# Windowed attention, then a sine-squared feed-forward layer: the squares of four groups of batch 0's first product move to GpSimd

## Chip, cores and metric

The kernel runs on one core of a Trainium2 chip. The metric is the device time of one execution in microseconds (us), as the median of several runs. A profile of one more execution shows what each engine did: TensorE (PE, its weight loads PEld), VectorE (DVE), ScalarE (ACT), GpSimd (POOL) and SyncE (SP, which issues transfers).

## What is computed

Eight batches of eight heads, 576 positions and 64 columns go through attention in which a position sees its neighbours within 32 and eight global positions; the result (4608 tokens x 512) goes through a layer with 2048 inner columns and a sine-squared activation.

```python
B, H, S, D = q.shape                       # 8, 8, 576, 64
scores = scale * np.matmul(q, k.transpose(0, 1, 3, 2))
mask = (np.abs(pos[:, None] - pos[None, :]) <= 32) | is_global[:, None] | is_global[None, :]
attn = softmax(np.where(mask, scores, -1e9))
x = (attn @ v).transpose(0, 2, 1, 3).reshape(B * S, H * D)
h = x @ w_in                               # 4608 x 2048
s = np.sin(alpha * h)
g = h + s * s / (alpha + 1e-09)
return (g @ w_out).astype(np.float32)
```

## The kernel before

The work goes batch by batch, in an order that is written out by hand (a manual schedule: each engine executes its instructions in the order of the program text, and waits at the head of its queue for what it needs). For batch b there is a stage of attention (`phase_a`, `attention`), then the first product with the activation (`gemm1`), and the second product (`gemm2`), whose matrix products are handed out piece by piece (`fill`) among the next batch's attention and first product.

`gemm1(b)` loops over 16 groups `nt` of 128 inner columns. For each group TensorE makes eight products (four row blocks of the weights, two halves of the 576 columns) into a PSUM bank pair; the groups take the bank pairs zn, zr and zd in turn, so that the product of group nt reuses the bank of group nt - 3. Then four steps follow: ScalarE's sine (L1162, bank to `sb`), the square (`sb` to `s2`: on ScalarE at L1165 if the group is in `on_act`, otherwise on VectorE at L1167), and VectorE's update (L1168), which multiplies the square by `recipT`, adds the bank and writes `H2`. With the update the bank is free again. `sb` and `s2` have three buffers each. For batch 0 `on_act` is `ON_ACT_FIRST`, the groups 1, 3, 5, 7, 9, 11, 13 and 14.

During batch 0's first product, the queries and keys of batch 1 are brought into their layout as well. Behind the products of the groups in `TURNED` (4, 7, 10, 13) TensorE transposes one pair of heads (`turn_lying`, L630) into the two spare PSUM banks zo. At the start of the groups in `PLACED` (5, 8, 11, 14), ahead of that group's sine in each queue, these banks are copied out (`place_lying`): the keys by VectorE (L637, into KX), the queries by ScalarE (L642, into QX). The next transposes into a bank wait for its copy.

GpSimd's queue in this stage holds, from group 1 on, two casts of the gathered rows of global keys and queries (L717, each waits for its gather), the issue of a transfer that casts batch 2's queries (L334, `cast_heads`), and from group 13 on three copies of global columns (`place_globals`, L374 and L377), which wait for two casts that VectorE makes behind group 12's transposes (`turn_kq`, L731). In the next stage its first instruction is a copy of one element that paces transfers (L353) and waits for the first masked weights E.

The next stage begins with seven products of `gemm2(0)` (L1220) into the spare bank from which the last keys were copied, followed by scores (L814) into a new bank pair in zr's place and into zd, exponentials on ScalarE (L822) and masks on VectorE (L831).

```python
ON_ACT_FIRST = (1, 3, 5, 7, 9, 11, 13, 14)
TURNED, PLACED, GLOBALS = (4, 7, 10, 13), (5, 8, 11, 14), 12
START = 7                                   # gemm2's products ahead of the next batch's scores
```

Of the kernel before, what the change touches and what calls it, by code (L numbers as in the profile page):

```python
# [10 lines left out]
ALU = mybir.AluOpType  # L11
# [238 lines left out]
def kernel(  # L250
# [11 lines left out]
    nc = tc.nc  # L262
# [68 lines left out]
    def cast_heads(b, src, name):  # L331

        cast[b, name] = dramp.tile([S, H, D], DT.bfloat16, name=name)
        nc.gpsimd.dma_start(out=cast[b, name][:], in_=src[b].rearrange("h s d -> s h d"))  # L334
# [16 lines left out]
    def pace(src):  # L351

        nc.gpsimd.tensor_copy(out=seen[0 : src.shape[0]], in_=src)  # L353

    def turn_k(b, _):
        kd = cast[b, "kd"][:].rearrange("a i h d -> a (i h d)")
        nc.sync.dma_start_transpose(out=KXt[b % 2][:].rearrange("p i h d -> p (i h) d")[:, :, 0:KT], in_=kd)
# [24 lines left out]
    def globals_of(b, rows, y):  # L382

        q0 = QX[b % 2][rows, :, y, PAD : PAD + 4]
        return bass.AP(
            tensor=q0.tensor, offset=q0.offset, ap=[list(q0.ap[0]), [2 * QROW, NHP], [SEG, 7], [1, 4]]
        )
# [14 lines left out]
    def load_v(b):  # L402

        src = cast[b, "vd"][:].rearrange("(m a) h d -> a m (h d)", a=KT)
        for half in range(2):
            m0 = half * (NT6 - 1)
            nc.sync.dma_start(
                out=VX[b % 2][half * D : half * D + KT].rearrange("p m h d -> p m (h d)"),
                in_=src[:, m0 : m0 + NT6 + 1],
            )  # L410

    def load_vg(b):
        for r in (KT, D + KT):
            nc.sync.dma_start(
                out=VX[b % 2][r : r + NG].rearrange("p m h d -> p m (h d)"),
                in_=VGb[b::B][:, None, :].to_broadcast([NG, NT6 + 1, H * D]),
            )
# [74 lines left out]
    for t in (gidx8, gp64):  # L492
        nc.vector.memset(t[:].bitcast(DT.int32), 0)
    nc.sync.dma_start(
        out=g64[:],
# [4 lines left out]
    for t in (0, D):  # L500
        nc.sync.dma_start(out=gp64[t + KT : t + NK], in_=global_idx[:, None])
        nc.sync.dma_start(
            out=gidx8[t + KT : t + NK],
# [31 lines left out]
    for i, bits in enumerate((B - 1, D - 1, B * (NG - 1))):  # L535
        nc.vector.tensor_scalar(
            out=rowi[:, i : i + 1], in0=prow[:], scalar1=bits, scalar2=None, op0=ALU.bitwise_and
# [12 lines left out]
        out=rowf[0 : NG * B, 4:5], in0=rowf[0 : NG * B, 0:1], scalar=float(S), in1=rowf[0 : NG * B, 3:4], op0=ALU.mult, op1=ALU.add  # L550
# [4 lines left out]
        out=of_batch[:], in0=rowf[0 : NG * B, 0:1], scalar1=0.0, scalar2=None, op0=ALU.is_equal  # L555
    )
    nc.vector.tensor_scalar(
        out=pick[:], in0=place8[0 : NG * B], scalar1=rowf[0 : NG * B, 2:3], scalar2=of_batch[:, 0:1],
# [8 lines left out]
    def warm(z, n):  # L567
# [9 lines left out]
        out=KX[1][:, :, :, NK:D], in_=zero[:][:, None, None, :].to_broadcast([P, NHP, NT12, D - NK]), func=AF.Copy,  # L577
# [15 lines left out]
    for half in range(2):  # L593
# [12 lines left out]
        out=band[:], in0=qrel[:], scalar1=float(WIN * WIN) + 0.5, scalar2=None, op0=ALU.is_le  # L606
    )
    for e, c0 in ((0, PAD), (1, 40)):
        nc.vector.tensor_copy(
            out=band[:, e, :, c0 : c0 + 4], in_=iskey[:, :, None].to_broadcast([P, 2, 4])  # L610
# [3 lines left out]
        out=M2, in_=band[:].rearrange("p e x c -> p e (x c)")[:, None].to_broadcast([P, NT6 // 2, 2, WCOL])  # L614
# [20 lines left out]
    def place_lying(b, w, hp, z, copy):  # L635
        if w == 1:
            copy(  # L637
                out=KX[b][:, hp, :, 0:KT].rearrange("p i (q r) -> p i q r", r=NR),
                in_=z.rearrange("p (r i q) -> p i q r", i=NT12, r=NR),
            )  # L640
        else:
            copy(  # L642
                out=QX[b][:, hp, :, PAD : PAD + 6 * SEG].rearrange("p y (m c) -> p y m c", c=SEG)[
                    :, :, :, 4:
                ].rearrange("p y m (e a) -> p y m e a", a=NR // 2),
                in_=z.rearrange("p (a y m e) -> p y m e a", y=2, m=6, a=NR // 2),
            )
# [11 lines left out]
        out=first[:], in0=gf[:], scalar1=gpf[:, 0:1], scalar2=None, op0=ALU.not_equal  # L659
# [3 lines left out]
        out=later[:], in0=jrow[:], scalar1=pm, scalar2=float(-KT), op0=ALU.subtract, op1=ALU.is_ge  # L663
# [8 lines left out]
    for w, name in ((1, "k"), (0, "q")):  # L672
        for t in range(2):
            nc.tensor.matmul(
                out=pg[w][t * D : (t + 1) * D], lhsT=g0[name][:], rhs=identb[0 : NG * B, t : NG * B : 2],
# [6 lines left out]
        out=KX[0][:, :, :, KT:NK],  # L682
        in_=pg[1].rearrange("p (j h) -> p h j", h=NHP)[:, :, None, :].to_broadcast([P, NHP, NT12, NG]),
    )
    for y in range(2):
        act(
            out=globals_of(0, slice(0, P), y),
# [6 lines left out]
        out=far[:], in0=qpos[:], scalar1=float(WIN * WIN) + 0.5,  # L694
# [20 lines left out]
    def cast_globals_kq():  # L715
        for w, src in ((1, gk), (0, gq)):
            nc.gpsimd.tensor_copy(out=gkq[w][:], in_=src)  # L717
# [26 lines left out]
    def halves(z, W):  # L744
        c = columns(z, W)
        return [(c[:, lo:hi], lo, hi) for lo, hi in ((0, HALF), (HALF, W))]
# [335 lines left out]
    TURNED, PLACED, GLOBALS = (4, 7, 10, 13), (5, 8, 11, 14), 12  # L1082
# [14 lines left out]
    def gemm1(b):  # L1097


        while len(waiting) > 1:  # L1100
            fill(1)
        xT = xTs[b]
        r0 = (b % 2) * S
        more = b == B - 1
        W = SG if more else S
        hr = tc.alloc_tile_pool(name="hr", bufs=1, space=PSUM)
        hs = {}

        def chunks(nt, cs, parts=slice(0, 2)):
            if nt not in hs:  # L1110
                hs[nt] = (zn, None, zd)[nt % 3] or hr.tile([P, 2, 512], DT.float32, name="zr")
            h = hs[nt]
            for c in cs:
                for h_part, lo, hi in halves(h, W)[parts]:
                    nc.tensor.matmul(  # L1115
                        out=h_part, lhsT=w_in[:, c, nt * P : (nt + 1) * P], rhs=xT[:, c, lo:hi],
                        start=(c == 0), stop=(c == CT - 1), skip_group_check=True,
                    )

        on_act = (ON_ACT_FIRST, ON_ACT_SECOND, ON_ACT)[min(b, 2)]  # L1120
        for nt in range(NT):
            at_group[0] = (b, nt)
            if b == 0 and nt in PLACED:
                hp = PLACED.index(nt)
                for w, copy in ((1, nc.vector.tensor_copy), (0, nc.scalar.copy)):
                    place_lying(1, w, hp, spare_banks[w], copy)
            if b == 0 and nt == 1:
                cast_globals_kq()
                load_v(1)
                load_vg(1)  # L1130
                cast_heads(2, q, "qd")
            if 0 < nt and cast_at.get((b, nt)):
                pace(H2[0:1, nt - 1, r0 : r0 + 1])
                for piece in cast_at[b, nt]:
                    cast_one(*piece)
            if 0 < b and b + 1 < B and 0 < nt <= TURNS:
                turn_k(b + 1, nt - 1)
            if 0 < b and b + 1 < B and nt == (LATE if b == 1 else TURNS + 1):
                load_v(b + 1)
                load_vg(b + 1)  # L1140
            if b == 0 and nt == GLOBALS + 1:
                for part in range(3):
                    place_globals(1, part, nc.gpsimd.tensor_copy)
            if more and nt == SOON:
                put_globals(slice(0, SOON))
            if nt == 0:

                for n in range(2):
                    chunks(n, range(CT - 1), slice(0, 2 - more))
                for n in range(2 * more):  # L1150
                    chunks(n, range(CT - 1), slice(1, 2))
            chunks(nt, range(CT - 1, CT) if nt < 2 else range(CT))
            h = columns(hs[nt], W)
            fill((GROUP_LAST if more else PER_GROUP)[nt])
            if nt and copied[0] == (b, nt - 2):
                fill(AFTER_COPY)
            if b == 0 and nt in TURNED:
                turn_lying(1, TURNED.index(nt), spare_banks)
            if b == 0 and nt == GLOBALS:
                turn_kq()  # L1160
            sb = spool.tile([P, SG], DT.bfloat16, name="sb")
            nc.scalar.activation(out=sb[:, 0:W], in_=h, func=AF.Sin, scale=alphaT[:, nt : nt + 1])  # L1162
            s2 = spool.tile([P, SG], DT.bfloat16, name="s2")
            if nt in on_act:
                nc.scalar.activation(out=s2[:, 0:W], in_=sb[:, 0:W], func=AF.Square)  # L1165
            else:
                nc.vector.tensor_tensor(out=s2[:, 0:W], in0=sb[:, 0:W], in1=sb[:, 0:W], op=ALU.mult)  # L1167
            nc.vector.scalar_tensor_tensor(  # L1168
                out=H2[:, nt, r0 : r0 + W], in0=s2[:, 0:W], scalar=recipT[:, nt : nt + 1], in1=h,
                op0=ALU.mult, op1=ALU.add,  # L1170
            )
        hr.release()
        at_group[0] = None
# [106 lines left out]
    def fill(n):  # L1280
        while n and waiting:
            if next(waiting[0], None) is None:
                waiting.pop(0)
            else:
                n -= 1
# [111 lines left out]
```

## Time and profile before

| what | us |
|---|---|
| median of three runs | 338.68 (338.3 to 339.26) |
| the profiled execution, its own time | 338.49 |
| its span, first to last instruction | 336.8 |
| batch 0's first product: first sine to last update | 31.46 to 53.45 |
| mean granted TensorE clock | 0.996 of full speed |

In the profile's rows, a group is written as output<-inputs by the names of the program's tiles; "x8" is a count, and the bracket at the end of a timeline row gives the idle time of the engine before it and what ended it. Of the columns of a timeline the first is the start in us from the span's beginning, the second the duration. The engine columns of the table by stretches are busy time with the number of instructions. In a table of groups the two numbers behind the bar are total busy time in us and the mean in ns. Spans on GpSimd are rough.

### The profile page before, as it was taken

The numbers are of one execution on the slowest core, as the hardware profiler recorded it, in microseconds if no ns is written. First come the engines' busy times: TensorE is split into PE (matmuls) and PEld (weight loads), VectorE is DVE, ScalarE is ACT, GpSimd is POOL, SyncE is SP. The second block draws the span as 40 slices with busy tenths as digits, with TensorE's granted clock in tenths as the row PEclk, the third lists the DMA queues.
The fourth block names the chain that finished last, engine by engine and source line by source line (L and its number), as shares of the span: only waits on it lengthen the run. The fifth ranks groups of instructions, "written<-read, shape, count | busy, mean of one in ns | idle before, by whom it ended". The sixth has DMA issues, their size and how long they took to land.

```text
span 336.8 us, 11878 instructions
## 1 busy us (share of the span) xinstructions
PE 316.2 (94%) x4812; PEld 202.8 (60%) x4812; DVE 255.9 (76%) x488; ACT 277.1 (82%) x402; POOL 143.7 (43%) x296
## 2 busy tenths in 40 slices
PE   0778999999999999999999999999999999999993
PEld 0765765577556765667556755676567745665553
DVE  4885896887887788688877788778868888788930
ACT  6775888989998889988998889889898898889611
POOL 7983324349516670666355652487060000004500
PEclk9999999999999999999999999999999999999998
DMA  7999999999989998999969993899999311010232
GB/s 104 114 162 205 186 226 169 152 166 135 181 143 133 190 124 137 94 119 186 151 93 137 172 162 85 131 176 136 132 111 133 65 60 42 1 33 8 73 93 69
DMA packets 141942, 42.01 MB, mean 125 GB/s; under 512 B 126426, under 2 KB 136794, under 8 KB 141882
## 3 DMA queue, kind: packets, MB, share of 16 engines
q0 software_dynamic: 100096, 18.51, 71.1%
q1 hardware_dynamic: 41786, 22.69, 34.1%
q8 instruction: 38, 0.62, 0.8%
q14 instruction: 22, 0.18, 0.2%
HBM read 41.95 MB, written 20.77 MB: 186 GB/s over the span
## 4 chain that ended last, share of the span: by engine, by line
PE 87%; DVE 4%; ACT 3%; issue 2%; DMA 1%; POOL 1%; DVEq 0%; POOLq 0%
PE zo L1220 38%; PE zn L1115 14%; PE zr L1115 11%; PE zd L1115 10%; PE ring L814 4%; PE zd L862 4%; PE zn L862 2%; DVE H L1168 2%; DMA g0k<-in_k_dram,grow 1%; ACT sb L1162 1%; PE zn L814 1%; PE zr L862 1%; DVE recipT L712 1%; DVE s L1167 1%; PE zo L630 1%
## 5 line engine op out<-in xcount | busy, mean ns | idle before, releaser
L1220 PE MATMUL zo<-w_out,H 128*128 128x512 bf16 (+1 forms) x576 | 147.1, 377 | 0.3 <-DVE KX L637 0.3
L1115 PEld LDWEIGHTS <-w_in 128*128 128x128 bf16 x1024 | 100.1, 98 | 43.9 <-issue 8.3
L1220 PEld LDWEIGHTS <-H 128*128 128x128 bf16 x592 | 53.7, 98 | 46.2 <-issue 0.4
L1115 PE MATMUL zn<-xT,w_in 128*128 128x288 bf16 (+1 forms) x384 | 57.7, 290 | 1.6 <-DVE H L1168 1.4
L1115 PE MATMUL zr<-xT,w_in 128*128 128x288 bf16 x320 | 48.0, 288 | 0.3
L1168 DVE SCALAR_TENSOR_TENSOR H<-s,recipT,zn 128x576 bf16<-128x576 bf16 (+1 forms) x48 | 39.4, 822 | 10.4 <-ACT s L1165 6.5
L1162 ACT ACTIVATE sb<-zn,alphaT 128x576 bf16<-128x576 f32 (+1 forms) x48 | 35.7, 743 | 13.7 <-PE zn L1115 13.2
L1115 PE MATMUL zd<-xT,w_in 128*128 128x288 bf16 x320 | 46.3, 288 | 0.3 <-DVE H L1168 0.2
L822 ACT ACTIVATE E<-ring 128x720 bf16<-128x720 f32 x46 | 35.9, 780 | 8.3 <-PE ring L814 7.7
L1167 DVE TENSOR_TENSOR s<-sb 128x576 bf16<-128x576 bf16 (+1 forms) x70 | 32.6, 465 | 12.2 <-ACT sb L1162 12.0
L1165 ACT ACTIVATE s<-sb 128x576 bf16<-128x576 bf16 (+1 forms) x58 | 40.0, 689 | 1.8
L831 DVE TENSOR_TENSOR E<-E,MASKT 128x720 bf16<-128x720 bf16 x64 | 33.5, 529 | 7.6 <-ACT E L822 5.6
L1168 DVE SCALAR_TENSOR_TENSOR H<-s,recipT,zd 128x576 bf16<-128x576 bf16 (+1 forms) x40 | 32.9, 822 | 7.6 <-ACT s L1165 5.0
L1168 DVE SCALAR_TENSOR_TENSOR H<-s,recipT,zr 128x576 bf16<-128x576 bf16 (+1 forms) x40 | 32.9, 822 | 6.6 <-ACT s L1165 5.0
L344 POOL DMA_DIRECT2D kd<-in_k_dram x48 | 31.4, 657 | 10.4 <-issue 8.0
L1162 ACT ACTIVATE sb<-zd,alphaT 128x576 bf16<-128x576 f32 (+1 forms) x40 | 29.6, 740 | 5.2 <-PE zd L1115 5.1
L1162 ACT ACTIVATE sb<-zr,alphaT 128x576 bf16<-128x576 f32 (+1 forms) x40 | 29.6, 740 | 4.3 <-PE zr L1115 4.3
L1210 POOL COPY H<-H 128x11 bf16 (+1 forms) x16 | 7.2, 453 | 57.6 <-DVE H L1168 56.7
L346 POOL DMA_DIRECT2D vd<-in_v_dram x48 | 30.5, 645 | 1.7 <-issue 1.3
L346 POOL DMA_DIRECT2D qd<-in_q_dram x40 | 25.4, 635 | 6.0 <-issue 6.0
L1227 ACT COPY osb<-zo 128x512 f32<-128x512 f32 (+1 forms) x33 | 19.1, 580 | 10.6 <-PE zo L1220 7.0
L814 PEld LDWEIGHTS <-KX 64*64 64x64 bf16 x896 | 15.8, 112 | 19.4 <-issue 19.0
(171 smaller groups left out, 377.7 us busy)
## 6 DMA issues: line engine op xcount, KB each, us to landing
VF<-vd SPq DMA_DIRECT2D x14, 336.0 KB
kd<-in_k_dram POOLq DMA_DIRECT2D x48, 72.0 KB, 4.8
vd<-in_v_dram POOLq DMA_DIRECT2D x48, 72.0 KB, 4.1
qd<-in_q_dram POOLq DMA_DIRECT2D x40, 72.0 KB, 5.5
w_out<-in_moe_w_out_dram POOLq DMA_DIRECT2D x2, 1024.0 KB, 25.7
out_dram<-osb SPq DMA_DIRECT2D x7, 256.0 KB
out_dram<-osb SPq DMA_DIRECT2D x8, 224.0 KB
out_dram<-osb SPq DMA_DIRECT2D x8, 192.0 KB
```

Of the source, the lines that this page charges most:

```text
L344: nc.gpsimd.dma_start(out=dst[:, :, h], in_=src.rearrange("(i a) d -> a i d", a=KT))
L346: nc.gpsimd.dma_start(out=dst[:, h], in_=src)
L814: nc.tensor.matmul(out=z[half * D : (half + 1) * D, t, 0 : G3 * WCOL].rearrange("p (m x c) -> p m x c", x=2, c=60)[:, m % G3, :, c0:c1], l ...
L822: nc.scalar.activation(out=weights(hp, g), in_=z[:, :, 0 : G3 * WCOL], func=AF.Exp, scale=scale)
L831: nc.vector.tensor_tensor(out=Eg, in0=Eg, in1=MASKT[:, None, G3 * g : G3 * (g + 1), :].rearrange("p o m c -> p o (m c)").to_broadcast([P, ...
L862: nc.tensor.matmul(out=nd(hp, key)[t * D : (t + 1) * D, half, :, a - half * CUT : z - half * CUT], lhsT=ones[rows, 0:D] if key else values ...
L1115: nc.tensor.matmul(out=h_part, lhsT=w_in[:, c, nt * P : (nt + 1) * P], rhs=xT[:, c, lo:hi], start=(c == 0), stop=(c == CT - 1), skip_group ...
L1162: nc.scalar.activation(out=sb[:, 0:W], in_=h, func=AF.Sin, scale=alphaT[:, nt : nt + 1])
L1165: nc.scalar.activation(out=s2[:, 0:W], in_=sb[:, 0:W], func=AF.Square)
L1167: nc.vector.tensor_tensor(out=s2[:, 0:W], in0=sb[:, 0:W], in1=sb[:, 0:W], op=ALU.mult)
L1168: nc.vector.scalar_tensor_tensor(out=H2[:, nt, r0 : r0 + W], in0=s2[:, 0:W], scalar=recipT[:, nt : nt + 1], in1=h, op0=ALU.mult, op1=ALU.add,)
L1220: nc.tensor.matmul(out=ops[:, cols], lhsT=H2[:, nt, blk * P : (blk + 1) * P], rhs=w_out[:, nt, cols], start=(nt == 0), stop=(nt == NT - 1) ...
```

## The change

In batch 0's first product, the groups of `PLACED` (5, 8, 11 and 14) take their square on GpSimd, as a multiplication of `sb` with itself. Before, the squares of 5, 11 and 14 were ScalarE's and that of 8 VectorE's. All other groups, all other batches and the order of the program text stay as they were.

```diff
             s2 = spool.tile([P, SG], DT.bfloat16, name="s2")
-            if nt in on_act:
+            if b == 0 and nt in PLACED:
+                nc.gpsimd.tensor_tensor(out=s2[:, 0:W], in0=sb[:, 0:W], in1=sb[:, 0:W], op=ALU.mult)
+            elif nt in on_act:
                 nc.scalar.activation(out=s2[:, 0:W], in_=sb[:, 0:W], func=AF.Square)
             else:
                 nc.vector.tensor_tensor(out=s2[:, 0:W], in0=sb[:, 0:W], in1=sb[:, 0:W], op=ALU.mult)
```

## The prediction

> **What bounds the kernel now.** I read the page first, then busy time in four stretches around the change, then the timeline of that stretch engine by engine. On the page I looked at the shares and at the chain that ended last.
>
> ```profile
> span 336.8 us, 11878 instructions
> PE 316.2 (94%) x4812; PEld 202.8 (60%) x4812; DVE 255.9 (76%) x488; ACT 277.1 (82%) x402; POOL 143.7 (43%) x296
> PE 87%; DVE 4%; ACT 3%; issue 2%; DMA 1%; POOL 1%; DVEq 0%; POOLq 0%
> ```
>
> Over the whole span TensorE is the bound, and GpSimd, idle for 57% of it, looks like a free helper. That is an average. The change lies in one stage, the first product of batch 0, and its stretches read differently:
>
> ```profile
> core 0: us, PE busy (x) PEld busy (x) DVE busy (x) ACT busy (x) POOL busy (x), PEclk, DMA share, GB/s
> 36.30:53.50 17.20, 16.25 (x300) 11.43 (x301) 16.40 (x25) 15.84 (x25) 4.56 (x5) 1.00 1.50 204
> 53.50:67.00 13.50, 13.50 (x349) 7.45 (x349) 9.49 (x20) 12.00 (x20) 6.66 (x12) 1.00 1.71 148
> 67.00:92.00 25.00, 24.70 (x226) 16.40 (x230) 20.46 (x35) 22.41 (x32) 16.87 (x36) 1.00 1.58 163
> ```
>
> From 36.30 to 53.50 VectorE is busy 16.40 of 17.20 us, TensorE 16.25, ScalarE 15.84: three engines are nearly full, and whatever is late shows. From 53.50 on TensorE is busy all the time (13.50 of 13.50, then 24.70 of 25.00), so a delay handed over at 53.5 meets no idle TensorE time in which it could be made up. The same row caps a gain: TensorE stands idle 17.20 - 16.25 = 0.95 us in this stage, so no relief of the other engines there can bring more.
>
> VectorE's queue, in its order. L1168 is the update that takes a group's square and gives its PSUM bank back (H<-s), L1167 a square, L637 a copy of transposed keys, L731 the two casts of turned globals (the first shown), L831 a mask of the next stage:
>
> ```profile
> 38.36 0.75 DVE L637 COPY KX<-zo 128x576 bf16<-128x576 bf16 x1
> 39.03 0.81 DVE L1168 SCALAR_TENSOR_TENSOR H<-s,recipT,zd 128x576 bf16<-128x576 bf16 x1
> ...
> 42.56 0.45 DVE L1167 TENSOR_TENSOR s<-sb 128x576 bf16<-128x576 bf16 x1
> 43.12 0.82 DVE L1168 SCALAR_TENSOR_TENSOR H<-s,recipT,zd 128x576 bf16<-128x576 bf16 x1
> ...
> 46.65 0.81 DVE L1168 SCALAR_TENSOR_TENSOR H<-s,recipT,zd 128x576 bf16<-128x576 bf16 x1
> 47.38 0.42 DVE L731 CAST kTg<-zo 128x256 bf16<-128x256 f32 x1
> ...
> 48.05 1.00 DVE L1167 TENSOR_TENSOR s<-sb 128x576 bf16<-128x576 bf16 x1
> 49.08 0.81 DVE L1168 SCALAR_TENSOR_TENSOR H<-s,recipT,zn 128x576 bf16<-128x576 bf16 x1
> ...
> 50.53 0.75 DVE L637 COPY KX<-zo 128x576 bf16<-128x576 bf16 x1
> 51.36 0.81 DVE L1168 SCALAR_TENSOR_TENSOR H<-s,recipT,zd 128x576 bf16<-128x576 bf16 x1
> ...
> 52.64 0.81 DVE L1168 SCALAR_TENSOR_TENSOR H<-s,recipT,zn 128x576 bf16<-128x576 bf16 x1
> 54.15 1.20 DVE L831 TENSOR_TENSOR E<-E,MASKT 128x720 bf16<-128x720 bf16 x2 [0.70 <-ACT E L822]
> ```
>
> The updates at 39.03, 43.12, 46.65 and 51.36 are those of groups 5, 8, 11 and 14. No wait stands in their rows: each square had been ready when VectorE came to it. All four hold the same bank, zd, since groups take zn, zr, zd in turn. So the product of group 8 waits for the update of 5, that of 11 for the update of 8, that of 14 for the update of 11: the four moved squares are in series, once around for every three groups.
>
> **The change, part by part.** It takes three squares (5, 11, 14) from ScalarE and one (8) from VectorE, and adds four to GpSimd. No DMA is moved. ScalarE's side, with the sines of groups 5, 8, 11, 14 and the square of 5:
>
> ```profile
> 37.41 0.74 ACT L1162 ACTIVATE sb<-zd,alphaT 128x576 bf16<-128x576 f32 x1
> 38.19 0.68 ACT L1165 ACTIVATE s<-sb 128x576 bf16<-128x576 bf16 x1
> ...
> 41.56 0.75 ACT L1162 ACTIVATE sb<-zd,alphaT 128x576 bf16<-128x576 f32 x1
> ...
> 45.16 0.74 ACT L1162 ACTIVATE sb<-zd,alphaT 128x576 bf16<-128x576 f32 x1 [0.20 <-PE zd L1115]
> ...
> 49.87 0.74 ACT L1162 ACTIVATE sb<-zd,alphaT 128x576 bf16<-128x576 f32 x1
> ```
>
> Removed: 3 x 0.68 us of ScalarE and 42.56 to 43.12 = 0.56 us of VectorE. ScalarE's gain I cost at nothing: what follows it (the next sine) waits for banks that the later updates give back, so it only gains idle time. VectorE's 0.56 us shorten the way to the update of 8, if that update isn't waiting for GpSimd instead.
>
> *The price of one square on GpSimd.* No GpSimd arithmetic with two inputs is in the trace. The nearest rows are copies there:
>
> ```profile
> L717 POOL CAST gkq<-SQ 64x512 bf16<-64x512 f32 x2 | 1.2, 606 | 7.3 <-DMA LC<-L 6.6 <-DMA SQ<-in_q_dram 0.7
> L353 POOL COPY seen<-xT 1x1 bf16<-1x1 bf16 x5 | 0.9, 178 | 0.0
> L374 POOL COPY KX<-kTg 128x384 bf16<-128x384 bf16 x1 | 0.9, 861 | 8.1 <-DVE kTg L731 8.1
> ```
>
> One element takes 178 ns, so that is the fixed part. The cast then runs at (606 - 178) / 512 = 0.84 ns an element of a row, the strided copy at (861 - 178) / 384 = 1.78. For 576 elements: 0.66 us if two inputs cost no more than one at the cast's rate (lower bound), 0.18 + 2 x 576 x 0.84 = 1.14 us if each input costs a pass, 1.20 us at the strided copy's rate for one pass, 2.23 us for two such passes (upper bound). I take 1.2 us, where the second and the third agree. That is against 0.68 on ScalarE and 0.45 on VectorE.
>
> [...]
>
> *What the square of group 5 is queued behind.* GpSimd's queue in this stretch, and an earlier issue of the same kind as its second row:
>
> ```profile
> 23.79 2.16 POOL L334 DMA_DIRECT2D vd<-in_v_dram  x1
> 25.48 1.34 POOL L432 DMA_DIRECT2D w_out<-in_moe_w_out_dram  x1
> ...
> 36.45 0.61 POOL L717 CAST gkq<-SQ 64x512 bf16<-64x512 f32 x1 [6.63 <-DMA LC<-L]
> 37.58 2.21 POOL L334 DMA_DIRECT2D qd<-in_q_dram  x1 [0.53 <-issue]
> 47.87 0.86 POOL L374 COPY KX<-kTg 128x384 bf16<-128x384 bf16 x1 [8.08 <-DVE kTg L731]
> 48.66 0.95 POOL L377 COPY QX<-qTg 128x112 bf16<-128x112 bf16 x2
> ```
>
> The idle GpSimd isn't idle where it is asked first. Since group 1 its queue has held a cast that waits for a gather (it starts at 36.45), and behind it the issue of batch 2's queries, 37.58 + 2.21 = 39.79. The sine of group 5 ends at 37.41 + 0.74 = 38.15, but its square can't start before 39.79 (39.27 if the next instruction may start 1.69 us into such an issue, as the pair at 23.79 and 25.48 has it). I take 39.79.
>
> *The sum.* Between an end and the start that it releases lie 0.04 to 0.07 us (the cast at 47.38 + 0.42 = 47.80, and the copy on GpSimd at 47.87); I take 0.08 from GpSimd back to VectorE.
>
> Group 5: 39.79 + 1.2 + 0.08 = 41.07 for the update, instead of 39.03: +2.04. Queued on VectorE behind it are the square and update of 6, the update of 7 and the key copy of 8, all late by as much; the update of 6 is waited for by the product of 9, that of 7 by the product of 10. The VectorE work up to the old place of square 8 is 42.56 - 39.03 = 3.53 us.
>
> Group 8, around the bank. TensorE's rows for a product on zd and for the end of the stage:
>
> ```profile
> 43.98 1.14 PE L1115 MATMUL zd<-xT,w_in 128*128 128x288 bf16 x8 [0.20 <-DVE H L1168]
> 51.34 1.67 PE L1220 MATMUL zo<-w_out,H 128*128 128x512 bf16 x7 [0.25 <-DVE KX L637]
> 53.13 0.33 PE L814 MATMUL zd<-QX,KX 64*64 64x120 bf16 x14
> ```
>
> Update 0.81, handover 0.05, product 1.14, handover 0.04, sine 0.74, handover 0.07, square 1.2, handover 0.08: 4.13 us from one update on zd to the next. That is more than VectorE's 3.53, so the 0.56 us taken off VectorE turn into waiting. Update of 8: 41.07 + 4.13 = 45.20, instead of 43.12: +2.08. Update of 11: 49.33, instead of 46.65: +2.68; here the old interval was 46.65 - 43.12 = 3.53 and the bank's round trip takes 0.6 more.
>
> From the update of 11 on, everything up to the last key copy hangs on VectorE's order: the two casts behind it, the transposes of group 13 that reuse the casts' bank, the copy at 50.53. All of it moves by +2.68. The three GpSimd copies stay behind these casts, as now.
>
> Group 14: the sine would end at 49.87 + 0.74 + 2.68 = 53.29, the square at 54.56, the update runs from 54.64 to 55.45. Who waits: the scores into zd, at 53.13 + 2.68 = 55.81. So a cover of 0.36 us is left, and group 14 costs nothing. The update of 15, behind it and its square (52.64 - 51.36 = 1.28 us later), ends at 56.73; the masks of the next stage wanted VectorE at 54.15 + 2.68 = 56.83. That cover is 0.1 us.
>
> TensorE's first output product waits for the last key copy: 51.34 + 2.68. From there it has no idle time to give. So +2.7 us on the profiled execution, whose own time is 338.49 us (span 336.8, and 1.69 around it), 0.19 below the median of 338.68. On the median: 338.68 + 2.7 = **341.4 us**.
>
> In general, with p for the price, the update of 11 comes at 39.87 + p + 2 x (2.93 + p), so the delay is 3p - 0.92; at 0.66 us +1.1, at 2.23 us +5.8; with GpSimd free at 39.27 half a us less.
>
> **The rivals.** *Not slower.* The mechanism: GpSimd is ready when the sine of 5 ends (38.22 with the handover), since the records on GpSimd are rough by the page's own word and the gather that heads its queue may land earlier, and a square costs little. The delay is then 3p - 2.49: below 1.0 us from p = 1.16 down, and at 0.66 about nothing (VectorE's queue is only 0.56 us shorter, and the rest of its order stays), so 338.7. For it: the pair at 23.79 and 25.48, with issues that overlap. Against: the two halves must come together, and the issue at 37.58 stands whole ahead of the square. Chance 0.13. Faster by over 1.0 us is excluded by TensorE's 0.95 us of idle time, short of something that isn't in these rows.
>
> *Dearer squares.* Two passes at the strided copy's rate, 2.23 us: +5.8 from the sum, and the update of 14 then ends at 50.61 + 5.8 + 0.07 + 2.23 + 0.08 + 0.81 = 59.6, past the scores at 53.13 + 5.8 = 58.9, so +6.5 and 345.2. For it: only that one 128-row copy has its rate. Against: the square's operands lie dense, as the cast's do. Chance 0.14.
>
> *VectorE and GpSimd hold each other up.* The square of 12 took 1.00 us at 48.05 instead of 0.45, beside the copies on GpSimd from 47.87 on. If a square on GpSimd costs its neighbour, or itself, as much, three rounds give 3 x 0.55 = 1.65 more: 343.0. Against: the update at 49.08 took its usual 0.81 while the copies at 48.66 ran for 0.95; and VectorE's own squares (6, 10, 12, 15) come behind the updates that wait for GpSimd, so they don't run beside its squares. Chance 0.11. [...]
>
> **How the numbers follow.** The forecast has 0.62, the rivals 0.13, 0.14 and 0.11. Its own range, for prices from 0.9 to 1.6 us and GpSimd free from 39.27 to 39.79, is +1.3 to +3.9: 340.0 to 342.6. To hold 8 in 10 the range reaches over the mutual hold-up and some way to either other rival: 339.5 to 344.0. A measurement of this kernel tells about 0.3%, 1.0 us, from no change. Slower by more: the forecast, both dear cases and some of the cheap one's upper end, 0.88. Within: 0.10. Faster: 0.02, for what the rows don't show.
>
> **What would show it.** On the timeline after: four GpSimd rows of L1165 at near 1.2 us each, the first right behind the issue of qd; the updates of 5, 8, 11 with a wait on GpSimd before them, at about 41.1, 45.2 and 49.3; a TensorE wait of nearly 2 us ahead of the product of 8; the first output product near 54.0 with its wait still on the key copy; ScalarE with more idle time in the stage, not less work on the chain; and from there each stage as long as before. It is wrong if the square of 5 starts at 38.2, if a square takes under 0.7 us or over 1.7, if the first output product comes by less than 1 us later, or if a later stage is shorter than before.

## The result and the profile after

| kernel | median of its runs, us (lowest to highest) | profiled execution, us | ratio to before, 95% interval |
|---|---|---|---|
| before, 8 runs | 338.69 (338.11 to 340.08) | 338.49 | |
| changed, 8 runs | 343.06 (341.41 to 345.30) | 343.01 | 1.0115 (1.0087 to 1.0143) |

The changed kernel is slower by 1.15%, 3.9 us by the ratio and 4.4 us between the medians, where 2.7 us was forecast. The page of the changed kernel, its first two parts and the shares of the chain:

```profile
span 341.2 us, 11815 instructions
PE 311.5 (91%) x4753; PEld 203.3 (60%) x4812; DVE 256.0 (75%) x487; ACT 275.6 (81%) x399; POOL 147.7 (43%) x300
PE 76%; ACT 7%; DVE 7%; issue 5%; DMA 2%; POOL 2%; DVEq 0%; POOLq 0%; ACTq 0%
```

VectorE has one instruction less, ScalarE three, GpSimd four more. TensorE's weight loads are all there (4812), but 59 of its products have no record (4753), so its lower busy time and part of the larger "issue" (5% instead of 2%) are gaps in the record, not in the work. The stage itself, as the same stretch of the table by stretches and as GpSimd's and VectorE's timelines:

```profile
36.30:53.50 17.20, 15.40 (x316) 11.19 (x316) 14.27 (x22) 13.46 (x21) 8.31 (x8) 1.00 1.51 207
```

```profile
35.67 0.61 POOL L717 CAST gkq<-SQ 64x512 bf16<-64x512 f32 x1 [6.11 <-DMA LC<-L]
36.82 2.20 POOL L334 DMA_DIRECT2D qd<-in_q_dram  x1 [0.54 <-issue]
39.11 1.15 POOL L1165 TENSOR_TENSOR s<-sb 128x576 bf16<-128x576 bf16 x1
43.25 1.15 POOL L1165 TENSOR_TENSOR s<-sb 128x576 bf16<-128x576 bf16 x1 [2.99 <-ACT sb L1162]
47.29 1.15 POOL L1165 TENSOR_TENSOR s<-sb 128x576 bf16<-128x576 bf16 x1 [2.90 <-ACT sb L1162]
...
52.57 1.15 POOL L1165 TENSOR_TENSOR s<-sb 128x576 bf16<-128x576 bf16 x1 [1.15 <-ACT sb L1162]
```

```profile
40.29 0.81 DVE L1170 SCALAR_TENSOR_TENSOR H<-s,recipT,zd 128x576 bf16<-128x576 bf16 x1 [0.31 <-POOL s L1165]
...
44.43 0.81 DVE L1170 SCALAR_TENSOR_TENSOR H<-s,recipT,zd 128x576 bf16<-128x576 bf16 x1 [0.65 <-POOL s L1165]
...
48.47 0.81 DVE L1170 SCALAR_TENSOR_TENSOR H<-s,recipT,zd 128x576 bf16<-128x576 bf16 x1 [0.56 <-POOL s L1165]
...
53.75 0.81 DVE L1170 SCALAR_TENSOR_TENSOR H<-s,recipT,zd 128x576 bf16<-128x576 bf16 x1 [0.65 <-POOL s L1165]
```

The stage began 0.87 us later than before, so the same stretch holds a slightly earlier piece of it. By its records TensorE stands still for 17.20 - 15.40 = 1.80 us of the stretch instead of 0.95; VectorE is busy for 14.27 us instead of 16.40, ScalarE for 13.46 instead of 15.84. All four squares take 1.15 us, and all four updates of the bank zd now wait for GpSimd. In this execution the first sine of the stage came at 32.33 instead of 31.46 (from 29.52 to 32.33 over all profiles below), and the gathers that head GpSimd's queue were done 0.78 us earlier (the cast at 35.67 instead of 36.45). The issue ahead of the square of 5 ended at 36.82 + 2.20 = 39.02, and so did its sine (38.28 + 0.74): the square started right behind both, and the queue cost nothing.

The rest is seen where the same instruction is compared in both kernels, late in the kernel. First before, then changed, from the timelines of TensorE and VectorE. The instructions are some denominators of batch 2's attention, an update of batch 3 and an output copy of batch 5:

```profile
96.12 0.49 PE L862 MATMUL zd<-E,ones 56*64 56x88 bf16 x28
96.55 1.25 PE L1220 MATMUL zo<-w_out,H 128*128 128x512 bf16 x5
...
150.50 0.81 DVE L1168 SCALAR_TENSOR_TENSOR H<-s,recipT,zn 128x576 bf16<-128x576 bf16 x1
...
212.73 0.69 DVE L1227 COPY osb<-zo 128x512 f32<-128x512 f32 x1
```

```profile
53.16 1.67 PE L1222 MATMUL zo<-w_out,H 128*128 128x512 bf16 x6 [0.25 <-DVE KX L637]
...
98.24 0.30 PE L862 MATMUL zd<-E,ones 56*64 56x88 bf16 x9
99.99 0.40 PE L862 MATMUL zd<-E,ones 56*64 56x120 bf16 x19 [1.45 <-issue]
100.32 1.25 PE L1222 MATMUL zo<-w_out,H 128*128 128x512 bf16 x4
...
154.57 0.81 DVE L1170 SCALAR_TENSOR_TENSOR H<-s,recipT,zn 128x576 bf16<-128x576 bf16 x1 [0.46 <-DVE s L1169]
...
217.17 0.69 DVE L1229 COPY osb<-zo 128x512 f32<-128x512 f32 x1 [0.45 <-DMA LC<-L]
```

The changed kernel is late by 53.16 - 51.34 = 1.82 us at the first output product (0.87 of it from before the stage, 0.95 from the stage), by 2.12 at the denominators, by 100.32 - 96.55 = 3.77 behind them, by 4.07 at the update and 4.44 at the copy; the spans differ by 4.4. A run of 28 equal products breaks after the ninth and goes on 1.45 us later, waiting for nothing that the profile names. VectorE stands idle for 0.46 and 0.45 us ahead of two instructions. The releasers named for them explain nothing: the first is VectorE's own square, which had ended 0.46 us before. None of that is in the stage that was changed: from first sine to first output product it lasts 20.83 us instead of 19.88, and the part behind it 288.1 instead of 285.4.

### The profile page after: what moved, and what is told of

Same layout as the page of the kernel before. It is cut to its first block, busy times and chain, and to the rows that moved or that the text cites. A ratio compares the mean times of both kernels' runs of the same rounds, so it can differ in the third digit from the quotient of the medians.

```text
span 341.2 us, 11815 instructions
## 1 busy us (share of the span) xinstructions
PE 311.5 (91%) x4753; PEld 203.3 (60%) x4812; DVE 256.0 (75%) x487; ACT 275.6 (81%) x399; POOL 147.7 (43%) x300
## 4 chain that ended last, share of the span: by engine, by line
PE 76%; ACT 7%; DVE 7%; issue 5%; DMA 2%; POOL 2%; DVEq 0%; POOLq 0%; ACTq 0%
PE zo L1222 32%; PE zn L1115 13%; PE zr L1115 10%; PE zd L1115 9%; PE ring L814 3%; DVE H L1170 3%; PE zd L862 3%; ACT sb L1162 3%; PE zn L862 2%; DMA H<-in_q_dram 2%; DVE s L1169 1%; ACT E L822 1%; ACT s L1167 1%; DVE xT L908 1%; ACT L L772 1%
## 5 line engine op out<-in xcount | busy, mean ns | idle before, releaser
L1222 PE MATMUL zo<-w_out,H 128*128 128x512 bf16 (+1 forms) x517 | 134.2, 376 | 6.1 <-issue 5.1
L1115 PE MATMUL zr<-xT,w_in 128*128 128x288 bf16 x320 | 48.8, 291 | 0.3
L1167 ACT ACTIVATE s<-sb 128x576 bf16<-128x576 bf16 (+1 forms) x55 | 37.9, 690 | 1.7
```

The source lines that it names most:

```text
L1115: nc.tensor.matmul(out=h_part, lhsT=w_in[:, c, nt * P : (nt + 1) * P], rhs=xT[:, c, lo:hi], start=(c == 0), stop=(c == CT - 1), skip_group ...
L1222: nc.tensor.matmul(out=ops[:, cols], lhsT=H2[:, nt, blk * P : (blk + 1) * P], rhs=w_out[:, nt, cols], start=(nt == 0), stop=(nt == NT - 1) ...
```

## The experiments

Four theories were in play, some of which the expectations give by letter or by a short name: that the price, GpSimd's queue and the bank's round trip make all of the delay (A); that the delay itself, whoever causes it, makes later stages longer (B); that GpSimd's work holds VectorE up (D, the prediction's third rival); and that the length of the instruction streams, VectorE's above all, and not the place of the squares, costs time later (E). "Stage" is the time from the first sine to the first output product, "rest" from there to the span's end, each in the profiled execution.

| kernel | median, us (lowest to highest, runs) | ratio to before, 95% interval | stage | rest | VectorE rows | break, us |
|---|---|---|---|---|---|---|
| again_before | 338.93 (338.6 to 340.32, 10) | 1.0015 (0.9998 to 1.0033) | 19.87 | 286.9 | 679 | 0.46 |
| again_after | 343.88 (342.59 to 346.14, 4) | 1.0135 (1.0092 to 1.0178) | 24.68 | 288.0 | 675 | 1.13 |
| only_5 | 342.63 (340.65 to 343.55, 6) | 1.0116 (1.0083 to 1.0150) | 21.08 | 285.9 | 678 | none |
| not_5 | 340.39 (338.98 to 340.94, 10) | 1.0034 (1.0012 to 1.0056) | 20.83 | 286.3 | 676 | none |
| queue_behind | 342.58 (342.04 to 343.18, 4) | 1.0113 (1.0077 to 1.0149) | 20.83 | 288.2 | 675 | 2.00 |
| before_queue_behind | 338.80 (338.06 to 340.53, 10) | 1.0002 (0.9973 to 1.0030) | 20.37 | 285.7 | 679 | none |
| plain_delay | 341.15 (339.71 to 343.11, 7) | 1.0062 (1.0025 to 1.0098) | 23.47 | 285.9 | 682 | none |
| idle_squares | 339.43 (338.34 to 341.04, 10) | 1.0017 (0.9994 to 1.0040) | 20.75 | 286.4 | 679 | none |
| after_padded | 341.65 (340.78 to 342.00, 4) | 1.0060 (1.0042 to 1.0078) | 22.20 | 286.3 | 678 | 1.07 |
| queue_behind_padded | 340.47 (339.10 to 341.74, 10) | 1.0032 (1.0006 to 1.0059) | 20.88 | 286.0 | 678 | 0.62 |
| after_padded_act | 343.15 (342.98 to 343.83, 4) | 1.0106 (1.0086 to 1.0125) | 21.91 | 288.7 | 675 | 1.72 |
| before_short | 341.19 (339.74 to 342.01, 5) | 1.0056 (1.0026 to 1.0085) | 19.86 | 286.5 | 675 | none |

"VectorE rows" counts its instructions with those that only wait on semaphores; "break" is TensorE's idle time within the run of 28 denominators shown above. The profile before has 679 such rows, a stage of 19.88, a rest of 285.4 and no break. The changed one has 675 (one square and three semaphore instructions fewer), 20.83, 288.1 and 1.45.

**again_before, again_after.** Both kernels once more, unedited.

> The kernel before, unchanged, for a second profile. Theory A (all of the loss is made in the changed stage, by the queue ahead of the first square and the round trip of the zd bank; the 2.6 us that the first profile after lost later is chance): the later stages of this profile differ from those of the first profile before by as much, up to 1 to 2 us in single places. Theory B (the stage's shift makes later stages longer): they agree within 0.5 us over the rest of the span. Both: 338 to 339.5 us.

> The changed kernel, unchanged, for a second profile. Theory A: the first output product of the next stage comes 1 to 2.7 us later, counted from the first sine of the stage, by when GpSimd gets free, and what is lost later is another amount in other places than the first time. Theory B: the loss after the stage is again near 2.6 us, with 1.5 us of it in the attention of batch 2. Both: 341.4 to 344 us.

The kernel before gave its own time again, though its profile has a rest of 286.9, with 0.46 us of TensorE's break: this part varies from one execution to the next. The changed kernel was as slow as the first time by the ratio, and its rest is 288.0, as long as the first time: theory A took the late loss for chance, and it isn't. Its profiled execution, at 346.14 us, shows another size of loss in the stage. Its rows on GpSimd, VectorE and TensorE, from the timeline, and three stretches around them (us, then busy time of TensorE, weight loads, VectorE, ScalarE, GpSimd, then granted clock):

```profile
40.68 1.65 POOL L1165 TENSOR_TENSOR s<-sb 128x576 bf16<-128x576 bf16 x1
...
42.36 0.82 DVE L1170 SCALAR_TENSOR_TENSOR H<-s,recipT,zd 128x576 bf16<-128x576 bf16 x1 [2.92 <-POOL s L1165]
...
43.23 1.14 PE L1115 MATMUL zd<-xT,w_in 128*128 128x288 bf16 x8 [2.76 <-DVE H L1170]
```

```profile
41.00:44.20 3.20, 0.97 (x8) 0.78 (x8) 1.73 (x3) 0.99 (x2) 1.33 (x2) 1.00 1.51 199
44.30:47.60 3.30, 3.15 (x15) 1.88 (x14) 2.37 (x4) 1.68 (x3) 1.15 (x1) 0.50 1.25 208
47.80:51.00 3.20, 3.20 (x87) 2.35 (x87) 2.73 (x4) 2.52 (x5) 0.39 (x1) 1.00 1.17 245
```

Here the gather landed late, so the square of 5 was held up and its update came 42.36 - 39.03 - 0.34 = 2.99 us later than before (0.34 is by how much this stage began later). TensorE stood still for 2.76 us, and behind that the granted clock was 0.50 for one stretch of 3.41 us: some fifteen products at half speed, which costs up to 1.7 us more (an estimate: half of 3.41). So the queue's price depends on when the gather lands (the cast behind it began at 37.80 here, at 35.67 in the first profile), and TensorE's wait of 2.76 us was paid for twice in this execution.

**only_5, not_5.** Only the square of group 5, or only those of 8, 11 and 14, on GpSimd.

```diff
-            if b == 0 and nt in PLACED:
+            if b == 0 and nt == 5:            # not_5: nt in (8, 11, 14)
```

> Only group 5's square on GpSimd; 11 and 14 go back to ScalarE, 8 to VectorE. Theory A: the square waits for the issue of the queries of batch 2; with GpSimd free 0.9 to 1.7 us after the sine the next stage starts 1.1 to 1.9 us later, and the time is 339.8 to 340.6. Rival C (the bank's round trip is all, the queue costs nothing): 0.3 us later, 339.0.

> Groups 8, 11 and 14 on GpSimd, 5 back on ScalarE. Theory A: no queue ahead of these; each of 8 and 11 adds 0.5 to 0.6 us by the bank's longer round trip, 14 nothing: the next stage starts 1.1 us later, 339.8. Rival C: as much as all four, so as the changed kernel. Theory B: 1.1 us in the stage and over 1 us more behind it, above 341.

The timeline of only_5, then that of not_5:

```profile
37.46 2.20 POOL L334 DMA_DIRECT2D qd<-in_q_dram  x1 [0.54 <-issue]
39.19 1.65 POOL L1165 TENSOR_TENSOR s<-sb 128x576 bf16<-128x576 bf16 x1
...
40.87 0.81 DVE L1170 SCALAR_TENSOR_TENSOR H<-s,recipT,zd 128x576 bf16<-128x576 bf16 x1 [1.26 <-POOL s L1165]
```

```profile
38.69 0.61 POOL L717 CAST gkq<-SQ 64x512 bf16<-64x512 f32 x1 [6.47 <-DMA LC<-L]
...
42.50 1.15 POOL L1165 TENSOR_TENSOR s<-sb 128x576 bf16<-128x576 bf16 x1 [0.46 <-ACT sb L1162]
43.69 0.81 DVE L1170 SCALAR_TENSOR_TENSOR H<-s,recipT,zd 128x576 bf16<-128x576 bf16 x1 [0.92 <-POOL s L1165]
```

In only_5 the square began 39.19 - 37.46 = 1.73 us into the issue ahead of it and its row spans 1.65: the two rows overlap, and the end comes where 2.20 and 1.15 in series would put it (37.46 + 2.20 + 1.15 = 40.81, measured 40.84). The queue is real: 1.26 us of VectorE's wait in the fastest execution of this kernel, whose stage is 1.2 us longer, as expected. Its median, 342.63, lies 2 us above the time expected: the other executions ran up to 2.9 us longer than the profiled one, and why isn't shown. Three of them, 342.70, 343.17 and 343.55 us, have a mean clock of 0.993 or 0.994 against 0.999 in one of 341.08 and 0.996 in the profiled one, whose clock fell only at its very end. In not_5 the cast came as late as 38.69 and hurt nobody: GpSimd then waits 0.46 us for the sine of 8. What is left is the round trip around the bank, +0.95 us in the stage and 1.0034 in time.

**queue_behind, before_queue_behind.** In the changed kernel and in the one before, the two casts of the gathered rows are put behind the square of group 5, so that nothing waits on GpSimd ahead of it (batch 2's query issue moves up to 29.84 with that).

```diff
 # at b == 0 and nt == 1
-                cast_globals_kq()
...
+            if b == 0 and nt == 6:
+                cast_globals_kq()
```

> All four squares on GpSimd, but the two casts that wait for the gathers stand behind group 5's square in GpSimd's queue, and the issue of batch 2's queries goes out ahead, at group 1. Theory A: the first square starts when its sine ends, the rest of the stage is the bank's round trip; from the first sine to the first output product 20.9 to 21.0 us instead of 19.9, no TensorE gap of 2 us, no half clock inside the stage; 339.6 to 340.2 us, if the same move alone costs nothing. Rival C (the queue costs nothing): as the changed kernel, above 342. Theory B (late loss whenever the stage is shifted): above 341.

> The kernel before with the same move of casts and issue, and no square on GpSimd: the control. All theories: 338.3 to 339.3 us, stage 19.9 us; if the earlier transfer of queries disturbs something, this shows it.

The timeline of queue_behind:

```profile
38.31 1.15 POOL L1166 TENSOR_TENSOR s<-sb 128x576 bf16<-128x576 bf16 x1 [6.26 <-ACT sb L1163]
...
52.36 1.67 PE L1223 MATMUL zo<-w_out,H 128*128 128x512 bf16 x6 [0.25 <-DVE KX L637]
```

The square waits for its sine alone, and the stage is down to 20.83 us. Yet the ratio stays at 1.0113: the rest is as long as in the changed kernel, 288.2. With no queue to blame, something else takes 288.2 - 285.4 = 2.8 us behind the stage. In the kernel before, the same move doesn't change the time (1.0002), though its stage, 20.37, is 0.5 us longer than expected.

**plain_delay.** The kernel before, with no square moved; VectorE makes one key copy of group 5 four times instead of once.

```diff
                     place_lying(1, w, hp, spare_banks[w], copy)
+                    for _ in range(3 if nt == 5 and w == 1 else 0):
+                        place_lying(1, w, hp, spare_banks[w], copy)
```

> The kernel before with VectorE's key copy of group 5 made four times instead of once: a delay of 3 x 0.73 = 2.2 us at the place where the changed kernel waits for its first square, with nothing on GpSimd. Theory A: 2.2 us, 340.8 to 341.0 in executions whose clock stays full. Theory B (a shifted stage loses more later, or lets the clock fall in its gap): 342.3 us or more, with the stall in batch 2's attention or a stretch of half clock in the profile.

Its stage is 3.6 us longer, and its rest 285.9, nearly that of before (285.4): this delay, handed over at 53 us, didn't make the rest longer by the 2.7 us of the changed kernel. It also repeats the clock's part. Two stretches of it:

```profile
37.90:41.20 3.30, 1.45 (x56) 1.26 (x56) 3.12 (x6) 1.89 (x3) 2.20 (x1) 1.00 2.26 168
41.30:44.60 3.30, 3.23 (x15) 1.87 (x13) 2.82 (x5) 1.59 (x3) 0.00 (x0) 0.50 1.27 207
```

TensorE was busy for 1.45 of 3.30 us, with no single gap over 1.90, and the next 3.41 us ran at half clock, as long as behind the gap of 2.76 us in again_after. A gap of 1.61 us in after_padded's stage left the clock at 1.00. What decides between these isn't shown.

**idle_squares.** The kernel before, and GpSimd squares `sb` of groups 8, 11 and 14 as well, into a tile that nobody reads: added work, and nothing waits for it.

```diff
+            if b == 0 and nt in (8, 11, 14):
+                s3 = spool.tile([P, SG], DT.bfloat16, name="s3")
+                nc.gpsimd.tensor_tensor(out=s3[:, 0:W], in0=sb[:, 0:W], in1=sb[:, 0:W], op=ALU.mult)
```

> The kernel before with three more squares, of groups 8, 11 and 14, made on GpSimd into tiles that nobody reads; the squares in use stay on VectorE and ScalarE. Theory A: the waiting is what costs, not the work: 338.4 to 339.0 us, where the same three in use cost 1.2 to 1.8. Rival D (GpSimd and VectorE hold each other up): VectorE's square of 8, and those beside, take about 1.0 instead of 0.45 us, and the time is 339.2 to 340.3.

GpSimd and VectorE on the timeline, both at the square of group 8:

```profile
40.65 1.15 POOL L1166 TENSOR_TENSOR s<-sb 128x576 bf16<-128x576 bf16 x1 [1.03 <-ACT sb L1162]
...
40.82 1.28 DVE L1170 TENSOR_TENSOR s<-sb 128x576 bf16<-128x576 bf16 x1
```

Side by side, VectorE's square takes 1.28 us instead of 0.45, while GpSimd's stays at 1.15: the hold-up of the third rival exists. In the changed kernel the two don't meet, so it doesn't make the loss. It isn't free: the product of group 11 waits for the late update of 8, and the stage is 20.75 us, 0.87 longer. The ratio of 1.0017 (0.9994 to 1.0040) doesn't tell this from nothing. The rest, 286.4, is within what the kernel before shows (285.4 and 286.9), so GpSimd's arithmetic doesn't bring the late loss either.

**after_padded, queue_behind_padded, after_padded_act.** What all kernels with a rest of 288 us share, among those told so far, is a VectorE stream of 675 rows. The first two add to the changed kernel and to queue_behind four one-element copies on VectorE and three on ScalarE; the third adds only ScalarE's.

```diff
+    pads = [main.tile([1, 2], DT.bfloat16, name=f"pad{i}") for i in range(2)]
...
+            if b == 0 and nt in (5, 11, 14):
+                nc.scalar.copy(out=pads[0][0:1, 0:1], in_=ones[0:1, 0:1])
+            for _ in range(4 if (b, nt) == (0, 8) else 0):       # not in after_padded_act
+                nc.vector.tensor_copy(out=pads[1][0:1, 0:1], in_=ones[0:1, 0:1])
```

> The changed kernel with three copies of one element on ScalarE (behind the sines of 5, 11, 14) and four on VectorE (in group 8), so that both engines have about as many instructions as before: 648 and 679 rows in the trace, where the changed kernel has 645 and 675. They write tiles that nobody reads. Theory E (the late loss comes from the length of the instruction streams: the transfers that bring instructions come at other places, TensorE's in the attention of batch 2 gets behind others, and it stands still for 1.4 to 2.3 us): the late loss of 2.4 to 3.1 us after the stage falls under 0.6, TensorE's 16 KB of instructions start at most 94.2 us (counted on the clock of the first profile) instead of 95.2; about 341 us instead of 343.5. Theory F (GpSimd's squares themselves, or the shift, cause the late loss): it stays, 343 us or more.

> The same seven copies in the version whose first square isn't queued behind the gathers and the issue. Theory E: only the bank's round trip is left, 1.0 us in the stage: 339.5 to 340.2 instead of 342.6. Theory F: 342.6 as without them.

> The changed kernel with ScalarE's three copies only. Theory E, with ScalarE's stream the one that matters: as with all seven, about 341 us; with VectorE's stream the one that matters: the late loss stays, 343 us or more. Theory F: 343 us or more.

The timeline of after_padded at the places of the late losses:

```profile
98.96 0.40 PE L862 MATMUL zd<-E,ones 56*64 56x120 bf16 x19 [1.07 <-issue]
99.29 1.25 PE L1228 MATMUL zo<-w_out,H 128*128 128x512 bf16 x4
...
153.15 0.81 DVE L1176 SCALAR_TENSOR_TENSOR H<-s,recipT,zn 128x576 bf16<-128x576 bf16 x1
...
215.37 0.69 DVE L1235 COPY osb<-zo 128x512 f32<-128x512 f32 x1
```

More work makes it faster: 1.0115 becomes 1.0060 and 1.0113 becomes 1.0032. VectorE's two idle times at 153 and 215 us are gone (late by 2.74 us at 99.29, by 2.65 and 2.64 behind), and TensorE's break is 1.07 instead of 1.45. The rest is still 0.9 us longer than before, where theory E expected under 0.6. ScalarE's copies alone don't do it: rest 288.7, ratio 1.0106. That is the cleanest pair, since after_padded, measured beside it on the same chip, differs by VectorE's four copies alone.

**before_short.** The other way round: the kernel before, all squares in their old places, but three constants and one small copy of the start-up made by GpSimd instead of VectorE.

```diff
-    nc.vector.memset(ones[:], 1.0)
+    nc.gpsimd.memset(ones[:], 1.0)
...                                          # zero, shift and the copy idf likewise
```

> The kernel before with four of VectorE's instructions of the set-up (three fills and a cast, all in the first microseconds) given to GpSimd: no square moved, the changed stage as it was, VectorE's stream four shorter. Theory E, VectorE's stream: the late loss appears without the change: TensorE stands still for over 0.7 us in batch 2's attention, the three small jumps of 0.2 to 0.4 us (second output product stage at 91, first products of batch 3 at 151 and batch 5 at 214) are there, and the time is 340.3 to 341.7. Theory F (only squares on GpSimd bring it about): 338.3 to 339.4, as the kernel before.

Its timeline at the same places:

```profile
96.50 0.61 PE L862 MATMUL zd<-E,ones 56*64 56x88 bf16 x28
...
151.28 0.81 DVE L1168 SCALAR_TENSOR_TENSOR H<-s,recipT,zn 128x576 bf16<-128x576 bf16 x1 [0.46 <-DVE s L1167]
...
213.88 0.69 DVE L1227 COPY osb<-zo 128x512 f32<-128x512 f32 x1 [0.45 <-DMA LC<-L]
```

Four VectorE instructions fewer, at the very start of the kernel, cost 1.0056 with the stage unchanged (19.86), and VectorE's idle times of 0.46 and 0.45 us stand ahead of the same two instructions as in the changed kernel. The kernel is late by 0.38 us at the denominators, 0.78 at the update and 1.15 at the copy. The break of over 0.7 us that was expected of TensorE is missing from this profile, which is the fastest of the five executions. The profile's rest, 286.5, is therefore no longer than again_before's; what speaks for a loss is the median and the place of the idle times. And GpSimd has four instructions more here, so VectorE's stream isn't all that differs.

**Where the idle times lie.** Counting VectorE's rows from the start of the trace, the idle instructions are the 192nd, the 320th and the 448th, both in the changed kernel and in before_short: 128 apart. Other stream lengths bring other instructions to these places, and the idle time goes with the place. From the timelines of the changed kernel, plain_delay (682 rows; its 192nd) and not_5 (676 rows; the 449th, behind a semaphore instruction as the 448th):

```profile
90.26 0.82 DVE L1170 SCALAR_TENSOR_TENSOR H<-s,recipT,zd 128x576 bf16<-128x576 bf16 x1 [0.46 <-DVE s L1169]
```

```profile
86.32 0.81 DVE L1170 SCALAR_TENSOR_TENSOR H<-s,recipT,zd 128x576 bf16<-128x576 bf16 x1 [0.46 <-DVE s L1169]
```

```profile
214.36 0.69 DVE L1229 COPY osb<-zo 128x512 f32<-128x512 f32 x1 [0.45 <-issue]
```

On the page, the queue q14 moves instructions in 22 transfers of 0.18 MB together, 8 KB each, and q8 in 38 of 0.62 MB, 16 KB each; TensorE has 4812 weight loads and as many products, 253 of its instructions to each of the 38. By that count 8 KB would be about 127 instructions (an estimate: half of 253), close to the 128 rows between VectorE's idle times; that a new block of its stream begins there is inferred from this. In the kernel before, the 192nd and the 320th row are semaphore instructions that come while an update still runs, 0.80 and 0.42 us before its end, and a change of block there would be covered; at the 448th it shows 0.14 us. Taken at 256 rows a transfer, an estimate (twice VectorE's 128, as 16 KB is twice 8 KB), TensorE's break lies close to the same count: the weight load behind it is the 3266th row of TensorE's stream, 13 x 256 - 62, as VectorE's 192nd is 2 x 128 - 64. The 16 KB transfer ahead of it begins later: the DMA view of the stretch 91 to 92 us before, then 97 to 98 us of the changed kernel:

```profile
q8 instruction: 1, 0.02, 7.7%
```

```profile
q8 instruction: 1, 0.02, 7.8%
```

Before, it starts 4 to 5 us ahead of the denominators at 96.12; after, at most 1.5 us ahead of the break, which begins at 98.24 + 0.30 = 98.54. The packets of q8 in the 14 traces show what the break goes with. In all seven profiles with a break, the weight load of row 3266 starts 1.26 to 1.47 us behind the end of this transfer (98.65 and 99.98 in the changed kernel). In plain_delay, before_short, only_5 and not_5 the load also follows it by 1.21 to 1.45 us, but the transfer came just in time, with pauses of 0.09 to 0.21 us. In the remaining three it had ended over 3 us ahead (at 92.65 before, for a load at 96.17), and there is no pause. So, by these 14 traces, TensorE stood still until its instructions had landed. VectorE's idle times are of another kind: they are 0.45 to 0.46 us each time, and no transfer of q14 ends in the 1.5 us ahead of any of them. At these counts the profile before shows 0.14 us of idle VectorE at one and no break of TensorE; in the changed kernel VectorE stood idle for 0.45 to 0.46 us at three of them and TensorE for 1.45 us at one.

## Why the prediction was right, and where it failed

*Direction, size and range* held: slower, +3.9 us by the ratio where +2.7 was forecast, and 343.06 us in a range of 339.5 to 344.0. But the size is made up otherwise than the sum had it, and that it fell into the range is in part luck. Of the 4.4 us between the two profiled spans, 0.87 came before the stage, 0.95 in it, where 2.7 were forecast, and 2.6 behind it, where nothing was. Counted from the stage's first sine, the square of 5 started at 39.11 - 0.87 = 38.24 and the first output product came 0.95 us later: two of the signs by which the prediction called itself wrong (38.2, and less than 1 us) are met in this profile.

*The price*, forecast 1.2 us: 1.15 in every undisturbed row. The dearer squares (2.23) are refuted.

*The bank's round trip*, forecast 4.13 us: 44.43 - 40.29 = 4.14 and 48.47 - 44.43 = 4.04. This step was right, and not_5 shows it by itself. Group 14 costs nothing, and the first output product still waits for the key copy (0.25), both as forecast.

*The queue ahead of group 5* was mis-sized because it isn't one number. Forecast +2.04 for the update of 5; measured +0.39 in the changed kernel (40.29 against 39.03 + 0.87), +1.34 in only_5 (40.87 against 39.03 + 0.50), +2.99 in again_after. It hangs on when the gather lands against the sine of 5, and the cast behind that gather began anywhere from 35.33 to 38.69 us in the profiles. In the changed kernel's profile GpSimd was free just when the sine ended, the mechanism of the first rival. Its formula, 3 x 1.15 - 2.49 = 0.96, is what the stage lost, 0.95; only the price wasn't low enough for that to come out as no change.

*"From there each stage as long as before"* is the step that failed: the rest became 2.6 us longer. The reason given, that TensorE has no idle time in which to make up a delay, was true, but it says nothing of new losses. The padded kernels take 0.0055 and 0.0081 off the ratio (1.9 and 2.7 us), and before_short brings 1.9 us with no square moved. In the changed kernel's profile VectorE's three idle times make it 0.30, 0.30 and 0.37 us later, and TensorE's wait for its instructions 1.45. Neither GpSimd's arithmetic (idle_squares), nor the queue (queue_behind), nor the delay as such (plain_delay) makes it.

*The clock* was in no step. It stayed at 1.00 in the stage of the changed kernel's profile, where TensorE's longest gap was 0.76 us; in again_after, where TensorE waited for 2.76 us, half clock took up to 1.7 us more, by the estimate above.

*Mutual hold-up* showed where both engines squared at once, which the waits of this change exclude, as argued; in idle_squares, where nothing excludes it, VectorE's square of group 8 took 1.28 us instead of 0.45 and the stage is 0.87 us longer.

So the runs show that a late loss comes without any moved square, that lengthening VectorE's stream by four instructions takes most of one away, and that TensorE's break ended 1.26 to 1.47 us behind the landing of its instructions each time. That block boundaries make VectorE's idle times rests on the count of 128, which holds for three stream lengths (675, 676 and 682 rows). Open stays why the transfer for TensorE starts when it does: it begins 3.6 to 4.1 us behind the weight load one block earlier (row 3010) in the four profiles of changed kernels with 675 rows, and at most 2.7 us behind it in the other ten. GpSimd's and ScalarE's streams changed in length too. Giving ScalarE its three instructions back had no effect (after_padded_act), and three more on GpSimd alone brought no late loss (idle_squares); before_short's four more on GpSimd weren't tried by themselves. That only_5 is as slow as all four squares together, and slower than after_padded, isn't settled either: they ran on different chips, with the gather landing at different times. No version was faster than the kernel before.

## What to carry to other kernels

Before giving work to an idle engine, read what stands at the head of its queue when the work comes up, and follow the buffer around: a square of 1.15 us instead of 0.68 made the time between two updates of its bank 4.04 us instead of 3.53 here, and the cast behind the gather, ahead of the first square in GpSimd's queue, began anywhere from 35.33 to 38.69 us. When a kernel loses time far from the edit, compare the same instruction in both traces at several places, find the jumps, and see whether they sit ahead of instructions that wait for nothing, and whether an instruction transfer has just ended there; then lengthen or shorten an engine's stream by a few tiny instructions before believing any story about the edit itself.

## What the hardware showed that was not expected

- Time was lost at fixed counts of the instruction streams. VectorE stood idle for 0.45 to 0.46 us ahead of its 192nd, 320th and 448th rows in the changed kernel, and TensorE broke once for 0.46 to 2.00 us (again_before, queue_behind), until 1.26 to 1.47 us behind the end of a 16 KB instruction transfer, in seven of 14 profiles. Four instructions more on VectorE went with 0.55 and 0.81% less time (after_padded, queue_behind_padded, with three more on ScalarE), four fewer with 0.56% more (before_short, with four more on GpSimd).
- TensorE's clock was half for 3.41 us behind a gap of 1.90 us with sparse work around it (1.45 us busy of 3.30, plain_delay) and behind one of 2.76 us (again_after); behind one of 1.61 us in after_padded it stayed full.
- VectorE's square of group 8, with both inputs from `sb`, took 1.28 us instead of 0.45 beside a GpSimd square, whose own time stayed at 1.15 (idle_squares).
- A GpSimd square whose row starts inside a transfer's issue had a row of 1.65 us instead of 1.15 (only_5, again_after); it ended where issue and square in series would have, at 40.84 us against 40.81 in only_5.
